# A lane convolution made two units ahead, and its VectorE part moved to one unit ahead

## The chip, the core and the metric

The kernel runs on one core of a Trainium2 chip. The metric is the device time of one execution, in microseconds (us). The kernel before took 767.79 us (median of three runs, 767.70 to 768.71).

The core's engines work side by side and meet through semaphores: TensorE (PE in the profile; its weight loads PEld) multiplies matrices into PSUM accumulators, VectorE (DVE), ScalarE (ACT) and GpSimd (POOL) work element by element, and SyncE (SP) only issues transfers. GpSimd and ScalarE can issue transfers too. Each engine takes its instructions in the order in which the program gives them.

## The reference

```python
# x: (8, 4096, 192); weight: (8 heads, 7 taps); softmax over the taps of each head
out = np.einsum('hk,bskhg->bshg', w, x_unf)     # causal convolution along the sequence, 24 channels a head
x = out.reshape(32768, 192)
gate = np.maximum(x @ w_gate, 0.0)              # 192 -> 1536
val = x @ w_val                                 # 192 -> 1536
return gate * val @ w_out                       # 1536 -> 192, float32
```

Each output token of the convolution is a weighted sum of the token and the six before it, with seven weights for each of the eight heads. Then comes a gated feed-forward layer.

## The kernel before

**Units.** The eight sequences are taken as four pairs; the two of a pair sit on partitions 0 to 63 and 64 to 127, and the 192 channels in three chunks (`c`) of 64. A unit is 1024 tokens of both sequences of a pair, in two windows of 512; there are 16 units. `xc[u]` holds a unit's convolved input in float16, `[128, 3, 1024]`, from a pool of three buffers.

**What TensorE does in a unit.** `gate_val(u, w)` runs once for each window: for each of 12 blocks `f` of 128 hidden channels, twelve matmuls of 512 columns (L505), the gate's into one PSUM tile and the value's into another. ScalarE makes the gate's relu (L516, `gr`), VectorE multiplies it with the value (L517, `hT`). Then `project(u, ...)` multiplies by the output weights. Its four tiles `i` are the two windows by the two sequences. In the normal form a tile is made in two half passes (`half_pass`, L536, `turn` 0 and 1) that use the upper and the lower 64 rows of the array side by side. The second pass of a tile may only start when the first is over; that is passed on by an empty instruction on SyncE's queue:

```python
done = nc.sync.nop()
tc.add_manual_dep(done.ins, mm.ins.name, SYNC, reason="first turn over")
```

The order of the passes (tile, turn) is (0,0) (1,0) (0,1) (2,0) (1,1) (3,0) (2,1) (3,1). After its second pass a tile is evicted from PSUM (L573, by ScalarE; the last tile of a unit by ScalarE and VectorE in halves) and stored by a transfer on SyncE's queue (L574). Unit 0 uses another form: four tiles, each of 48 full-height matmuls (`half_whole`, L556), without the empty instructions. All PSUM tiles come from one pool of four.

**How a unit's convolution is made.** Unit 0 is convolved on TensorE with a dense form (`conv_dense`, L333), unit 1 with banded matmuls (`conv`, L358): a group of up to five blocks of 112 tokens takes eight matmuls of 48 columns a block, five moves by ScalarE out of PSUM (L373) and one transpose on SyncE's queue for each block into `xc[1]` (L395). Units 2 to 15 are made by the "lanes". The lane of a unit `u` is loaded by GpSimd (`lane_load`, L414), copied by GpSimd and turned by nine transposes on SyncE's queue (`lane_turn`, L433 and L436). Tokens 0 to 575 are made by VectorE: ScalarE writes the first tap's product (`lane_first`, L469), VectorE adds the other six taps for each chunk (`lane_rest`, L481, 18 steps, the last three writing `xc`). Tokens 576 to 1023 are GpSimd's: ScalarE and VectorE write the products of tap and token (`product`, L452 and L454), GpSimd adds them in six steps (`add`, L458), the last of which writes `xc`.

**Order.** The schedule is written by hand: the order of the Python calls is each engine's order. In the loop over `u`, the lane of unit `u + 2` is turned, VectorE's 18 steps and the products for unit `u + 2` stand behind the second window's gate and value work and so run during `project(u)`, and GpSimd's adds for unit `u + 1` run during unit `u`. So both parts of a unit are begun two units ahead, VectorE's part is also done two units ahead, and GpSimd's part one. Unit 1's ten blocks are convolved in two groups: group 2 ahead of `project(0)`, group 3 behind its first tile.

Of the kernel before, what the change touches and what calls it, by code (L numbers as in the profile page):

```python
# [8 lines left out]
FP = mybir.dt.float32  # L9
F16 = mybir.dt.float16  # L10
# [5 lines left out]
def kernel(  # L16
# [25 lines left out]
    SUB = 112  # L42
    VECTOR = [
        [(0, 5), (1, 5), (2, 5), (0, 4), (1, 4), (2, 4), (2, 1)],
        [(0, 5), (1, 5), (2, 5), (0, 6), (2, 1)],
    ]
# [11 lines left out]
    second = [min(t, 2 * UNIT - SUB) for t in range(UNIT, 2 * UNIT, SUB)]  # L58
    GROUPS += [(0, second[:GSUB]), (0, second[GSUB:])]
# [3 lines left out]
    xpool = ctx.enter_context(tc.tile_pool(name="xpool", bufs=3))  # L63
# [3 lines left out]
    ypool = ctx.enter_context(tc.tile_pool(name="ypool", bufs=2))  # L67
# [7 lines left out]
    def load_x(g):  # L75


        bp, toks = GROUPS[g]
        xt = xpool.tile([128, GSUB, 2, D], F16, name="x_h")
        rows, step = (SUB, DSUB) if g < 2 else (128, SUB)  # L80
        for st in range(2):
            b = bp + NB * st
            last = toks[-1] - toks[-2] != step
            n_full = len(toks) - int(last)
            src = bass.AP(
                tensor=x.tensor,
                offset=x.offset + (b * S + toks[0] - PAD) * D,
                ap=[[D, rows], [step * D, n_full], [1, D]],
            )
            nc.gpsimd.dma_start(out=xt[0:rows, 0:n_full, st, :], in_=src)  # L90
            if last:
                nc.gpsimd.dma_start(
                    out=xt[0 : SUB + PAD, len(toks) - 1, st, :],
                    in_=x[b, toks[-1] - PAD : toks[-1] + SUB, :],
                )
        return xt
# [305 lines left out]
    def lane_load(u):  # L402


        bp, t0 = u * UNIT // S, u * UNIT % S
        xe = epool.tile([128, TILES, 2, NCH, 64], F16, name="x_e")
        j0 = int(t0 == 0)
        if j0:
            nc.gpsimd.memset(xe[0:HALO, 0, :, :, :], 0.0)
        for st in range(2):  # L410
            b = bp + NB * st
            for j, n in ((j0, TDVE - j0), (TDVE, TILES - TDVE)):
                lo = t0 - HALO + 128 * j if j < TDVE else t0 + LDVE - HALO
                nc.gpsimd.dma_start(  # L414
                    out=xe[:, j : j + n, st, :, :].rearrange("p j c r -> p j (c r)"),
                    in_=bass.AP(
                        tensor=x.tensor,
                        offset=x.offset + (b * S + lo) * D,
                        ap=[[D, 128], [128 * D, n], [1, D]],
                    ),  # L420
                )
            if j0:
                nc.gpsimd.dma_start(
                    out=xe[HALO:128, 0, st, :, :].rearrange("p c r -> p (c r)"),
                    in_=x[b, 0 : 128 - HALO, :],
                )
        xes[u] = xe

    def lane_turn(u):
        xe = xes.pop(u)  # L430
        xp = epool.tile([128, TILES, NCH, 2, 64], F16, name="x_p")
        for st in range(2):
            nc.gpsimd.tensor_copy(out=xp[:, :, :, st, :], in_=xe[:, :, st, :, :])  # L433
        xr = rpool.tile([128, NCH, 128 * TILES], F16, name="x_r")
        for j in range(TILES):
            nc.sync.dma_start_transpose(  # L436
                out=xr[:, :, 128 * j : 128 * j + 128],
                in_=xp[:, j].rearrange("p c s r -> p (c s r)"),
            )
        xrs[u] = xr  # L440

    def shifted(u, c, k, lane):
        o = HALO - KW + 1 + k
        if lane:
            return xrs[u][:, c, 128 * TDVE + o : 128 * TDVE + o + LPOOL]
        return xrs[u][:, c, o : o + LDVE]

    def product(engine, u, c, k):
        out = prods[u][:, k, c, :]
        in_, scale = shifted(u, c, k, 1), tap[:, c, k : k + 1]  # L450
# [5 lines left out]
    def add(u, k):  # L456
        pr = prods[u]
# [7 lines left out]
    def lane_first(u):  # L465
        accs[u] = apool.tile([128, NCH, LDVE], FP, name="acc")
        xc[u] = xcpool.tile([128, NCH, UNIT], F16, name="xc")
        for c in range(NCH):
            nc.scalar.activation(  # L469
                out=accs[u][:, c, :],  # L470
                in_=shifted(u, c, 0, 0),
                func=ACTF.Copy,
                scale=tap[:, c, 0:1],
            )
        prods[u] = apool.tile([128, KW, NCH, LPOOL], FP, name="prods")

    def lane_rest(u):
        acc = accs.pop(u)
        for k in range(1, KW):
            for c in range(NCH):  # L480
                nc.vector.scalar_tensor_tensor(  # L481
                    out=xc[u][:, c, 0:LDVE] if k == KW - 1 else acc[:, c, :],
                    in0=shifted(u, c, k, 0),
                    scalar=tap[:, c, k : k + 1],
                    in1=acc[:, c, :],
                    op0=ALU.mult,
                    op1=ALU.add,
                )
        for c, k in VECTOR[u > 2]:
            product(nc.vector, u, c, k)  # L490
# [62 lines left out]
    def half_whole(h, st, outs):  # L553
        for q in range(4):
            for f in range(NFF):
                nc.tensor.matmul(  # L556
                    out=outs[q],
                    lhsT=h[:, f, st, 128 * q : 128 * (q + 1)],
                    rhs=Wo[:, f, :],
                    start=(f == 0),  # L560
                    stop=(f == NFF - 1),
                )

# [44 lines left out]
    def project(u, hs, work):  # L608
# [3 lines left out]
        if u == 0:  # L612
            order = [(i, 2) for i in range(4)]
        if u == NUNIT - 1:
            order = [(0, 0), (1, 0), (0, 1), (2, 0), (1, 1), (2, 1), (3, 2)]
        for i, turn in order:
            h, st = hs[i // 2], i % 2
            row0 = (bp + NB * st) * S + WIN * (w0 + i // 2)
            if u == NUNIT - 1 and i == 3:
                last_half(h, st, row0)  # L620
                continue
            if turn in (0, 2):
                at[i] = slots()
            if turn in (1, 2):
                for c, k in work[i]:
                    product(nc.scalar, u + 2, c, k)
# [18 lines left out]
    lane_load(2)  # L645
    xts[2] = load_x(2)
    nc.gpsimd.dma_start(out=Wo[:], in_=moe_w_out.rearrange("(c p) d -> p c d", p=128))
    for u in range(NUNIT):
        lane = 1 <= u < NUNIT - 1
        if lane:  # L650
            add(u + 1, 1)
        if u == 1:
            lane_load(3)
            add(2, 2)
            add(2, 3)
# [5 lines left out]
        if u == 0:  # L661
            xts[3] = load_x(3)
        if 0 < u < NUNIT - 3:
            lane_load(u + 3)
        if lane:
            for k in range(4 if u == 1 else 2, KW - 1):
                add(u + 1, k)
        while len(hs) < 2:
            hs.append(gate_val(u, len(hs)))
        if lane:  # L670
            add(u + 1, KW - 1)
        if u == 0:
            xc[1] = xcpool.tile([128, NCH, UNIT], F16, name="xc")
            conv(2, 0)
            conv(2, 1)
        del xc[u]
        work = [[] for _ in range(4)]
        if u + 2 < NUNIT:
            lane_first(u + 2)
            lane_rest(u + 2)  # L680
            todo = [(c, k) for k in (0, 1, 2, 3, 4, 6) for c in range(NCH)]
            todo = [ck for ck in todo if ck not in VECTOR[u > 0]]
            cut = [0, 4, 8, 12, 16] if u == 0 else [0, 5, 10, 15, 16]
            work = [todo[a:b] for a, b in zip(cut, cut[1:])]
# [31 lines left out]
```

## Time and profile before

| | us |
|---|---|
| median of the runs before | 767.79 |
| the profiled execution | 767.88 |
| its span, first to last instruction | 765.9 |
| outside the span | 2.0 |

| engine | busy us | share of the span |
|---|---|---|
| TensorE, matmuls | 761.7 | 99% |
| VectorE | 692.7 | 90% |
| ScalarE | 600.7 | 78% |
| GpSimd | 369.9 | 48% |

A line of the profile gives the engine, the line of kernel.py, the operation, its output and inputs by the program's names, their shapes and the count. In the timeline the first two numbers are the start and the length of a merged row in us, and brackets tell how long the engine was idle before it and what released it. SPq is SyncE's queue of transfers. The ends of matmuls are modelled; they lie about 0.16 us behind the start of the next one.

### The profile page before, as it was taken

The page shows a single profiled execution, that of the slowest core. Times are in us where ns is not written, and L with a number is a line of the kernel's source. Part 1 is how long each engine was busy: PE and PEld are TensorE (multiplying, and loading weights), DVE is VectorE, ACT ScalarE, POOL GpSimd, SP SyncE. Part 2 cuts the span into 40 slices and gives each one's busy share as a digit, 9 for nine tenths or more (in the row PEclk, how much of TensorE's full clock was granted, in tenths as well). Part 3 has the DMA queues.
Part 4 walks back from the last instruction along what each step waited for, and adds up shares of the span by engine and source line. Part 5 has one row for each costly group of instructions (what it writes and reads, how often), then busy time and mean ns, then how long its engine had stood idle before and what let it go on. Part 6 is the DMA issues. An engine that isn't in the chain of part 4 may idle for free.

```text
span 765.9 us, 24782 instructions
## 1 busy us (share of the span) xinstructions
PE 761.7 (99%) x10794; PEld 502.5 (66%) x10794; DVE 692.7 (90%) x746; ACT 600.7 (78%) x735; POOL 369.9 (48%) x212
## 2 busy tenths in 40 slices
PE   9999999999999999999999999999999999999998
PEld 4595674946749476584755848567484674947648
DVE  7999999999999999999999999999999999996591
ACT  6797887878878787887878878788787887875571
POOL 8608648093570926619166290743908346090000
PEclk9999999999999999999999999999999999999999
DMA  8966727190472804528054281722919131200202
GB/s 121 134 104 116 92 91 88 54 122 6 100 78 66 110 23 97 61 85 95 23 111 47 85 92 44 106 31 85 93 44 117 21 92 39 65 22 15 71 2 84
DMA packets 131810, 56.12 MB, mean 73 GB/s; under 512 B 96741, under 2 KB 131701, under 8 KB 131701
## 3 DMA queue, kind: packets, MB, share of 16 engines
q1 hardware_dynamic: 90789, 38.85, 25.1%
q0 software_dynamic: 40768, 15.59, 18.9%
q8 instruction: 84, 1.38, 0.8%
q14 instruction: 25, 0.20, 0.1%
q10 hardware_dynamic: 144, 0.10, 0.0%
HBM read 31.68 MB, written 25.17 MB: 74 GB/s over the span
## 4 chain that ended last, share of the span: by engine, by line
PE 99%; DMA 1%; issue 0%; POOL 0%; ACT 0%; POOLq 0%
PE ps L505 65%; PE ps L536 31%; PE ps L556 2%; DMA x_h<-in_x_dram 1%; PE ps L594 1%; PE ps L333 0%; PE ps L358 0%; POOL spaced L129 0%; ACT acc L573 0%; POOLq L700 0%
## 5 line engine op out<-in xcount | busy, mean ns | idle before, releaser
L517 DVE TENSOR_TENSOR hT<-gr,ps 128x1024 f16<-128x1024 f16 (+1 forms) x386 | 468.9, 1215 | 37.0 <-ACT gr L516 9.9
L516 ACT ACTIVATE gr<-ps 128x1024 f16<-128x1024 f32 (+1 forms) x386 | 392.9, 1019 | 102.4 <-PE ps L505 100.6
L458 POOL TENSOR_TENSOR prods<-prods 128x1344 f32<-128x1344 f32 x70 | 212.4, 3034 | 309.1 <-DVE prods L454 305.7
L505 PE MATMUL ps<-xc,Wg 64*128 64x512 f16 x2304 | 311.9, 376 | 0.0
L505 PE MATMUL ps<-xc,Wv 64*128 64x512 f16 x2304 | 311.8, 376 | 0.0
L536 PEld LDWEIGHTS <-hT 64*128 64x128 f16 x5664 | 234.1, 94 | 3.6
L536 PE MATMUL ps<-Wo,hT 64*128 64x192 f16 x5664 | 236.1, 243 | 0.0
L505 PEld LDWEIGHTS <-Wv 64*128 64x128 f16 x2304 | 129.8, 94 | 118.5 <-DVE hT L517 0.3
L505 PEld LDWEIGHTS <-Wg 64*128 64x128 f16 x2304 | 112.2, 94 | 132.4 <-issue 0.2
L481 DVE SCALAR_TENSOR_TENSOR acc<-x_r,tap,acc 128x576 f32<-128x576 f16 x210 | 154.3, 811 | 1.6 <-ACT acc L469 1.6
L452 ACT ACTIVATE prods<-x_r,tap 128x448 f32<-128x448 f16 x222 | 130.3, 662 | 0.0
L573 ACT COPY out_s<-ps 128x768 f32<-128x768 f32 (+1 forms) x63 | 45.7, 725 | 52.4 <-PE ps L536 42.5
L414 POOL DMA_DIRECT2D x_e<-in_x_dram x56 | 45.1, 818 | 3.4 <-POOL x_p L433 3.4
L433 POOL COPY x_p<-x_e 128x1728 f16<-128x1728 f16 x28 | 44.7, 1624 | 1.7 <-DMA x_e<-in_x_dram 1.6
L458 POOL TENSOR_TENSOR xc<-prods 128x1344 f16<-128x1344 f32 x14 | 42.4, 3027 | 1.1
L481 DVE SCALAR_TENSOR_TENSOR xc<-x_r,tap,acc 128x576 f16<-128x576 f16 x42 | 31.8, 810 | 0.0
L573 DVE COPY out_s<-ps 128x384 f32<-128x384 f32 x15 | 8.3, 550 | 25.5 <-ACT out_s L573 25.5
L469 ACT ACTIVATE acc<-x_r,tap 128x576 f32<-128x576 f16 x42 | 29.4, 766 | 0.0
L454 DVE TENSOR_SCALAR prods<-x_r,tap 128x448 f32<-128x448 f16 x72 | 27.3, 446 | 0.0
L556 PE MATMUL ps<-Wo,hT 128*128 128x192 f16 x192 | 16.2, 246 | 0.0
L556 PEld LDWEIGHTS <-hT 128*128 128x128 f16 x192 | 15.9, 98 | 0.0
L90 POOL DMA_DIRECT2D x_h<-in_x_dram x6 | 4.9, 825 | 0.0
(54 smaller groups left out, 66.9 us busy)
## 6 DMA issues: line engine op xcount, KB each, us to landing
out_dram<-out_s SPq DMA_DIRECT2D x63, 384.0 KB
x_e<-in_x_dram POOLq DMA_DIRECT2D x34, 192.0 KB, 6.2
x_e<-in_x_dram POOLq DMA_DIRECT2D x22, 240.0 KB, 4.8
x_r<-x_p SPq DMA_TRANSPOSE x126
Wo<-in_moe_w_out_dram POOLq DMA_DIRECT2D x1, 576.0 KB
x_h<-in_x_dram POOLq DMA_DIRECT2D x2, 240.0 KB, 7.6
x_h<-in_x_dram POOLq DMA_DIRECT2D x2, 210.0 KB, 5.1
x_h<-in_x_dram POOLq DMA_DIRECT2D x2, 192.0 KB, 7.6
```

The source lines that it names most:

```text
L414: nc.gpsimd.dma_start(out=xe[:, j : j + n, st, :, :].rearrange("p j c r -> p j (c r)"), in_=bass.AP(tensor=x.tensor, offset=x.offset + (b ...
L433: nc.gpsimd.tensor_copy(out=xp[:, :, :, st, :], in_=xe[:, :, st, :, :])
L452: engine.activation(out=out, in_=in_, func=ACTF.Copy, scale=scale)
L458: nc.gpsimd.tensor_tensor(out=pr[:, 0] if k < KW - 1 else xc[u][:, :, LDVE:UNIT], in0=pr[:, 0], in1=pr[:, k], op=ALU.add,)
L469: nc.scalar.activation(out=accs[u][:, c, :], in_=shifted(u, c, 0, 0), func=ACTF.Copy, scale=tap[:, c, 0:1],)
L481: nc.vector.scalar_tensor_tensor(out=xc[u][:, c, 0:LDVE] if k == KW - 1 else acc[:, c, :], in0=shifted(u, c, k, 0), scalar=tap[:, c, k : k ...
L505: nc.tensor.matmul(out=pss[i][:, st, :], lhsT=W[64 * st : 64 * st + 64, c, 128 * f : 128 * (f + 1)], rhs=xcb[64 * st : 64 * st + 64, c, WI ...
L516: nc.scalar.activation(out=gr[:, sts], in_=pss[0][:, sts], func=ACTF.Relu)
L517: nc.vector.tensor_tensor(out=h[:, f, sts], in0=gr[:, sts], in1=pss[1][:, sts], op=ALU.mult)
L536: mm = nc.tensor.matmul(out=outs[q], lhsT=h[64 * r : 64 * r + 64, f, st, 128 * q : 128 * (q + 1)], rhs=Wo[64 * r : 64 * r + 64, f, :], sta ...
L556: nc.tensor.matmul(out=outs[q], lhsT=h[:, f, st, 128 * q : 128 * (q + 1)], rhs=Wo[:, f, :], start=(f == 0), stop=(f == NFF - 1),)
L573: one(out=dst[:, step * j : step * j + step], in_=src[:, step * j : step * j + step])
```

## The change

VectorE's part of a lane now belongs to the next unit, and GpSimd's to the one after it. The lane `v` holds tokens 0 to 575 of unit `v` and tokens 576 to 1023 of unit `v + 1`. In the loop over `u` lane `u + 1` is turned and worked on, so VectorE's part of unit `u + 1` is made during `project(u)`, and the products for GpSimd's part of unit `u + 2` too. GpSimd's adds in unit `u` make unit `u + 1`'s part, as before. Lanes run from 1 to 15; the last has no GpSimd part. On TensorE only tokens 576 to 1023 of unit 1 are convolved, in one group of four blocks. It is called in `project(0)` behind pass (1,1). Unit 0's projection takes the form of half passes that the other units have.

GpSimd's copies and SyncE's transposes of a lane are made for VectorE's five blocks first and then for GpSimd's four. The output weights are loaded ahead of unit 1's input. Two pools shrink: `xpool` from three buffers to two, `ypool` from two to one. The products that VectorE makes are the same five in each unit.

```diff
-    VECTOR = [
-        [(0, 5), (1, 5), (2, 5), (0, 4), (1, 4), (2, 4), (2, 1)],
-        [(0, 5), (1, 5), (2, 5), (0, 6), (2, 1)],
-    ]
+    VECTOR = [(0, 5), (1, 5), (2, 5), (0, 6), (2, 1)]
...
-    second = [min(t, 2 * UNIT - SUB) for t in range(UNIT, 2 * UNIT, SUB)]
-    GROUPS += [(0, second[:GSUB]), (0, second[GSUB:])]
+    GROUPS += [(0, list(range(UNIT + LDVE, 2 * UNIT, SUB)))]
...
-    def lane_load(u):
+    def pieces(v):
+        both = [(0, TDVE, v * UNIT)]
+        if v + 1 < NUNIT:
+            both.append((TDVE, TILES - TDVE, (v + 1) * UNIT + LDVE))
+        return both
...
+    def lane_turn(v):
+        xe = xes.pop(v)
+        xp = epool.tile([128, TILES, NCH, 2, 64], F16, name="x_p")
+        xr = rpool.tile([128, NCH, 128 * TILES], F16, name="x_r")
+        for j0, n, _ in pieces(v):
+            for st in range(2):
+                nc.gpsimd.tensor_copy(
+                    out=xp[:, j0 : j0 + n, :, st, :], in_=xe[:, j0 : j0 + n, st, :, :]
                 )
...
+            for j in range(j0, j0 + n):
+                nc.sync.dma_start_transpose(
+                    out=xr[:, :, 128 * j : 128 * j + 128],
+                    in_=xp[:, j].rearrange("p c s r -> p (c s r)"),
+                )
+        xrs[v] = xr
...
-            out=pr[:, 0] if k < KW - 1 else xc[u][:, :, LDVE:UNIT],
+            out=pr[:, 0] if k < KW - 1 else xc[v + 1][:, :, LDVE:UNIT],
...
-        if u == 0:
-            order = [(i, 2) for i in range(4)]
...
-            if turn == 2:
-                half_whole(h, st, at[i][1])
-            else:
-                done[i] = half_pass(h, st, at[i][1], turn, done.get(i))
+            done[i] = half_pass(h, st, at[i][1], turn, done.get(i))
             if turn:
-                evict(at[i][0], row0, u > 0 and i == 3 or u == NUNIT - 1 and i == 2)
-            if u == 0 and i == 0:
-                conv(3, 0)
-                conv(3, 1)
+                evict(at[i][0], row0, i == 3 or u == NUNIT - 1 and i == 2)
+            if u == 0 and (i, turn) == (1, 1):
+                conv(2, 0)
+                conv(2, 1)
...
-    lane_load(2)
+    lane_load(1)
+    nc.gpsimd.dma_start(out=Wo[:], in_=moe_w_out.rearrange("(c p) d -> p c d", p=128))
     xts[2] = load_x(2)
-    nc.gpsimd.dma_start(out=Wo[:], in_=moe_w_out.rearrange("(c p) d -> p c d", p=128))
     for u in range(NUNIT):
-        lane = 1 <= u < NUNIT - 1
-        if lane:
-            add(u + 1, 1)
...
+        adds = 1 <= u < NUNIT - 1
+        if u + 1 < NUNIT:
+            xc[u + 1] = xcpool.tile([128, NCH, UNIT], F16, name="xc")
+        if adds:
+            add(u, 1)
         hs = []
         if u == 0:
             hs.append(gate_val(0, 0))
+        if u + 1 < NUNIT:
+            lane_turn(u + 1)
         if u + 2 < NUNIT:
-            lane_turn(u + 2)
...
+            lane_load(u + 2)
+        if adds:
+            for k in range(2, KW):
+                add(u, k)
         while len(hs) < 2:
             hs.append(gate_val(u, len(hs)))
...
-            conv(2, 0)
-            conv(2, 1)
         del xc[u]
         work = [[] for _ in range(4)]
+        if u + 1 < NUNIT:
+            lane_first(u + 1)
+            lane_rest(u + 1)
         if u + 2 < NUNIT:
-            lane_first(u + 2)
-            lane_rest(u + 2)
...
         project(u, hs, work)
```

More of the change, by code (lines that the diff above doesn't have):

```diff
@@ L78, in load_x @@
         bp, toks = GROUPS[g]
+        n, rows, step = len(toks), SUB if g < 2 else 128, toks[1] - toks[0]
         xt = xpool.tile([128, GSUB, 2, D], F16, name="x_h")
-        rows, step = (SUB, DSUB) if g < 2 else (128, SUB)
         for st in range(2):
-            b = bp + NB * st
-            last = toks[-1] - toks[-2] != step
-            n_full = len(toks) - int(last)
             src = bass.AP(
                 tensor=x.tensor,
-                offset=x.offset + (b * S + toks[0] - PAD) * D,
-                ap=[[D, rows], [step * D, n_full], [1, D]],
-            )
[L90 to L95, printed above, removed]
+                offset=x.offset + ((bp + NB * st) * S + toks[0] - PAD) * D,
+                ap=[[D, rows], [step * D, n], [1, D]],
+            )
+            nc.gpsimd.dma_start(out=xt[0:rows, 0:n, st, :], in_=src)
         return xt
@@ L414, in lane_load @@
+    def lane_load(v):
+        xe = epool.tile([128, TILES, 2, NCH, 64], F16, name="x_e")
+        for j0, n, t in pieces(v):
+            bp, t0 = t // S, t % S
+            start = int(t0 == 0)
+            if start:
+                nc.gpsimd.memset(xe[0:HALO, j0, :, :, :], 0.0)
+            for st in range(2):
+                b = bp + NB * st
                 nc.gpsimd.dma_start(
-                    out=xe[:, j : j + n, st, :, :].rearrange("p j c r -> p j (c r)"),
+                    out=xe[:, j0 + start : j0 + n, st, :, :].rearrange("p j c r -> p j (c r)"),
@@ L442, in shifted @@
[L442 removed]
+                        offset=x.offset + (b * S + t0 - HALO + 128 * start) * D,
+                        ap=[[D, 128], [128 * D, n - start], [1, D]],
+                    ),
+                )
+                if start:
+                    nc.gpsimd.dma_start(
+                        out=xe[HALO:128, j0, st, :, :].rearrange("p c r -> p (c r)"),
+                        in_=x[b, 0 : 128 - HALO, :],
+                    )
+        xes[v] = xe
+    def lane_turn(v):
[3 more added lines that the diff above has]
+        for j0, n, _ in pieces(v):
+            for st in range(2):
+                nc.gpsimd.tensor_copy(
+                    out=xp[:, j0 : j0 + n, :, st, :], in_=xe[:, j0 : j0 + n, st, :, :]
+                )
+            for j in range(j0, j0 + n):
+                nc.sync.dma_start_transpose(
+                    out=xr[:, :, 128 * j : 128 * j + 128],
+                    in_=xp[:, j].rearrange("p c s r -> p (c s r)"),
+                )
+        xrs[v] = xr
@@ L443, in shifted, with product @@
+    def shifted(v, c, k, lane):
         o = HALO - KW + 1 + k
         if lane:
[L445 to L450, printed above, removed]
+            return xrs[v][:, c, 128 * TDVE + o : 128 * TDVE + o + LPOOL]
+        return xrs[v][:, c, o : o + LDVE]
+    def product(engine, v, c, k):
+        out = prods[v][:, k, c, :]
+        in_, scale = shifted(v, c, k, 1), tap[:, c, k : k + 1]
@@ L463, in add, with lane_first @@
         )
-    def lane_first(u):
-        accs[u] = apool.tile([128, NCH, LDVE], FP, name="acc")
-        xc[u] = xcpool.tile([128, NCH, UNIT], F16, name="xc")
+    def lane_first(v):
+        accs[v] = apool.tile([128, NCH, LDVE], FP, name="acc")
         for c in range(NCH):
             nc.scalar.activation(
-                out=accs[u][:, c, :],
-                in_=shifted(u, c, 0, 0),
+                out=accs[v][:, c, :],
+                in_=shifted(v, c, 0, 0),
                 func=ACTF.Copy,
@@ L474, in lane_first, with lane_rest @@
             )
-        prods[u] = apool.tile([128, KW, NCH, LPOOL], FP, name="prods")
-    def lane_rest(u):
-        acc = accs.pop(u)
+    def lane_rest(v):
+        acc = accs.pop(v)
         for k in range(1, KW):
@@ L481, in lane_rest @@
                 nc.vector.scalar_tensor_tensor(
-                    out=xc[u][:, c, 0:LDVE] if k == KW - 1 else acc[:, c, :],
-                    in0=shifted(u, c, k, 0),
+                    out=xc[v][:, c, 0:LDVE] if k == KW - 1 else acc[:, c, :],
+                    in0=shifted(v, c, k, 0),
                     scalar=tap[:, c, k : k + 1],
@@ L488, in lane_rest @@
                 )
-        for c, k in VECTOR[u > 2]:
-            product(nc.vector, u, c, k)
+        if v + 1 < NUNIT:
+            prods[v] = apool.tile([128, KW, NCH, LPOOL], FP, name="prods")
+            for c, k in VECTOR:
+                product(nc.vector, v, c, k)
     def gate_val(u, w):
@@ L551, in half_pass @@
             return done
[L553 to L562, printed above, removed]
     def put(copy, queue, src, row, n, gap, os_=None):
```

61 lines of the change are left out of this document (9 added, 52 removed).

## The prediction

> **What bounds the kernel now.** I read the page first (busy shares, the chain that ended last), then the chain in order of time, then the timelines of the engines around unit 0 and around unit 3, which stands for units 1 to 14.
>
> Page, parts 1 and 4:
>
> ```profile
> PE 761.7 (99%) x10794; PEld 502.5 (66%) x10794; DVE 692.7 (90%) x746; ACT 600.7 (78%) x735; POOL 369.9 (48%) x212
> PE 99%; DMA 1%; issue 0%; POOL 0%; ACT 0%; POOLq 0%
> ```
>
> TensorE is never without work: what lengthens or shortens its own chain is the whole answer, and everything else matters only if it makes TensorE wait. The chain in order of time (start, length, what) gives its stages:
>
> ```profile
> 21.57 19.56 PE ps L505 x180
> 41.13 0.99 PE ps L358 x8
> 42.12 3.96 PE ps L556 x48
> 46.09 0.82 PE ps L358 x8
> 46.91 11.88 PE ps L556 x144
> 58.79 31.19 PE ps L505 x288
> ...
> 183.81 15.84 PE ps L536 x384
> 199.66 31.08 PE ps L505 x288
> ```
>
> A unit is 31.08 us of gate and value matmuls (L505) and 15.84 us of projection (L536), 46.92 together, with no hole. Unit 0 differs: its projection is 3.96 + 11.88 in full-height matmuls (L556), with the two convolutions (L358, 0.99 and 0.82) between; from 41.13 to 58.79 that is 17.66 us. This stretch is what the change rewrites.
>
> **Units 1 to 15: a new wait, with cover.** VectorE's rows are now made in the unit before they are read, so the first gate matmuls of a unit wait for the last VectorE steps of the unit before. Timelines of VectorE and TensorE where unit 3 ends:
>
> ```profile
> 196.35 2.27 DVE L481 SCALAR_TENSOR_TENSOR xc<-x_r,tap,acc 128x576 f16<-128x576 f16 x3
> 199.49 0.81 PE L505 MATMUL ps<-xc,Wg 64*128 64x512 f16 x6
> ```
>
> The three final steps (one for each 64-channel chunk) end between 197.16 and 198.62. TensorE starts the next unit at 199.49 and comes to the third chunk four matmuls (0.43 us) later, at 199.92. The cover is 2.3 us for the first chunk and 1.30 for the third, in all units alike, since VectorE's order within a unit stays (15 + 3 steps, five products, half an eviction). I cost this wait at nothing. Behind it would stand all of TensorE; a lag beyond 1.30 us would be paid at each of 15 boundaries. Unit 14 gets 18 steps for unit 15 (13.3 us) where VectorE idled (14.77 us before its eviction, by its timeline). GpSimd's adds come in the same unit as before; its two copies of 1.62 us become four of 0.9 or 0.7, in a unit in which it waits over 20 us.
>
> **Start.** The loads keep their places on GpSimd's queue, but the output weights now go ahead of unit 1's input: they are needed at 41, were issued at 24.68, and the move brings them forward. The unit-1 input is needed ten us later than before. Nothing here is on the chain.
>
> **Unit 0, step by step.** I set 0 where the projection starts, and take ScalarE's times from its timeline of unit 3 (projection from 183.65; evictions of the first and second tile):
>
> ```profile
> 189.80 0.80 ACT L573 COPY out_s<-ps 128x768 f32<-128x768 f32 x1 [0.77 <-PE ps L536]
> 193.76 0.80 ACT L573 COPY out_s<-ps 128x768 f32<-128x768 f32 x1 [0.36 <-PE ps L536]
> ```
>
> The eight passes of a projection take 15.84 / 8 = 1.98 us each.
>
> *Convolution.* Sixteen matmuls of 240 columns (0.99 + 0.82 us) become eight of 192: 0.82 x 192/240 = 0.66 to 0.79, taken as 0.75. Half passes instead of full-height matmuls cost the same (15.84 both). On TensorE alone the stretch is 15.84 + 0.75 = 16.6: 1.1 less than 17.66.
>
> *The accumulator of the fourth tile.* The convolution's two accumulators come between the third and the fourth tile's, and there are four in all, so pass (3,0) now gets the second tile's and waits for its eviction. The second tile's pass (1,1) ends at 9.90, the convolution at 10.65, the eviction (193.76 + 0.80, less 183.65) at 10.91. (3,0) starts at about 11.0: 0.35 lost. (3,0) ends at 12.98, (2,1) at 14.96.
>
> *SyncE's queue.* This is the item that decides. Pass (3,1) may start only when SyncE has passed on the end of (3,0), by the empty instruction that `half_pass` puts on its queue. Between that and the instruction before it now stand the convolution's four transposes (`conv` is called behind pass (1,1), and `nc.sync` issues in order). Unit 0 had no such instruction before, as it used `half_whole`. What a transpose costs SyncE, and that what stands behind it waits, its timeline of unit 0 shows:
>
> ```profile
> 43.74 6.92 SPq L395 DMA_TRANSPOSE xc<-y  x5
> 50.76 0.53 SPq L574 DMA_DIRECT2D out_dram<-out_s  x1
> 51.39 8.21 SPq L395 DMA_TRANSPOSE xc<-y  x5
> 59.71 1.86 SPq L574 DMA_DIRECT2D out_dram<-out_s  x3
> ```
>
> The answer for line 395 (shortest/median/longest, ns) and ScalarE's timeline of the same unit:
>
> ```profile
> L395 SPq DMA_TRANSPOSE xc<-y x10: 1174/1246/1814, 43.7 to 58.4; - x10
> ```
>
> ```profile
> 47.82 0.81 ACT L573 COPY out_s<-ps 128x768 f32<-128x768 f32 x1
> 48.49 2.03 ACT L373 CAST y<-ps 112x480 f16<-112x480 f32 x5
> ```
>
> The first tile was evicted at 48.63, and its store, though ready, went out at 50.76, right behind five transposes; the later stores sat behind the second five until 59.71. So the queue is strictly in order, and a transpose holds it for 1.17 to 1.81 us. Stores could wait; TensorE can't.
>
> In the changed kernel ScalarE starts the five moves out of the convolution 0.69 after the start of the second eviction (48.49 - 47.82): at 10.80. They took 2.03 for 480 columns; for 384, 1.62: done at 12.45. Four transposes then take 5.1 at the median with 0.05 between, 5.7 with one of the long ones. Both groups of before had one of 1.81 among their first four, so I take 5.6: until 18.05. Another 0.1 to the next instruction of the queue (43.74 + 6.92 to 50.76), and as much again to TensorE, an estimate: (3,1) starts at 18.25 instead of 14.96, and ends at 20.23.
>
> *Sum.* 20.23 - 17.66 = +2.6; counted from starts of matmuls (41.0 to 58.72) it is +2.5. So 1.1 us of removed matmuls is paid back by 0.35 and 3.3 us of stall. Low end: median transposes, +2.0. High end: if unit 1's rows are turned no earlier than unit 2's were (the first product then at 45.58, and not 2.48 behind the start, at 43.5), ScalarE, with 0.36 to spare before the second eviction, is 1.7 late: +4.2. I take no lateness, since VectorE's five blocks are now loaded and copied first, so that SyncE can begin about two copies (1.8 us) after 25.7 rather than at 30.7. In the longer projection VectorE's rows for unit 1 (42.8 + 13.3 = 56.1) are in time; the convolved rows are read only in the second window, 15 us later.
>
> Nothing else moves the chain. The profiled execution took 767.88 (span 765.9), 0.09 above the median of the three runs, 767.79. 767.88 + 2.5 is 770.4; as a median 770.3.
>
> **Rivals.**
>
> *TensorE's clock falls in the stall.* Between (2,1) and (3,1) there are 3.3 us without a matmul. Before, no hole of this kind exists between 8 us and the end. At the very start the trace shows a slow pace:
>
> ```profile
> 0.86 2.83 PE L157 MATMUL ps<-const-bfloat16-1.0 128*128 128x512 bf16 x7 [0.86 <-PEq L700]
> ```
>
> Six matmuls of 512 columns and one of 128 take 2.83, 0.45 for 512 columns, where the gate has 31.08 / 144 = 0.216 for a pair that runs side by side. A further one at 4.09 is still 0.45 from the next start, 4.54; so some four us went at half pace, two us lost. The same after the stall would make it +4.5, 772.3. Against it: the hole is short, and there would be one only; the granted clock column reads 1.00 even at the start, so it tells nothing. [...]
>
> *The transposes don't hold (3,1): not slower.* If SyncE were through by 14.96, only the 0.35 would remain: 9.90 + 0.75 + 0.35 + 5.94 = 16.9, -0.7, a median of 767.1. That needs four transposes in 14.96 - 12.45 = 2.5 us, 0.63 each, about half of the shortest row, 1.17; above that every us more is a us of TensorE. [...] That the change doesn't do what it says is no way to this: the program's order has eight convolution matmuls of 192 columns, and the four transposes before the third store.
>
> *VectorE comes late at each boundary.* The price is 15 times what goes beyond 1.30 us: at 0.3 us over, +4.5, on top of the +2.5, 774.8. Against it stands that the ends repeat to 0.1 us in all units before.
>
> **How the numbers follow.** Stall in unit 0 as summed (769.8 to 772.0 with its bounds): 0.77. With the clock's fall: 0.08. Transposes hidden: 0.08. VectorE late: 0.03. Something not seen: 0.04, of it 0.03 faster. A measurement of this kernel can tell about 0.2%, 1.5 us, from no change; 770.3 is +0.33%, and the low end of the sum +0.26%. Slower: 0.77 + 0.08 + 0.03, less 0.03 for a stall shorter than its low end, 0.85. Same: 0.08 + 0.03 + 0.01 = 0.12. Faster: 0.03. The range leaves out the hidden transposes and the late VectorE: 769.2 to 772.4.
>
> **What would show it.** In the profile after: 46.92 us for units 1 to 14; in unit 0 one idle time of TensorE of some 3.3 us ahead of the last pass, released by SyncE, with four transposes on SyncE until just before it; 20.2 us from gate to gate there. No such hole, and the unit at 16.9, would prove the queue harmless; matmuls at twice their length behind the hole, the clock; a gate start that waits for VectorE, the third rival.

## The result and the profile after

The changed kernel took 775.22 us (median of five runs, 774.47 to 775.57) beside 768.18 for the kernel before on the same chip: the ratio is 1.0085, with an interval of 1.0074 to 1.0096. It is slower, as forecast, but by 7.0 us and not 2.5, and 2.8 us above the top of the range. The profiled execution took 774.75, span 772.9 (before: 767.88 and 765.9).

Parts 1 and 4 of the page of the changed kernel:

```profile
PE 763.0 (99%) x10978; PEld 506.0 (65%) x10978; DVE 705.4 (91%) x763; ACT 601.7 (78%) x735; POOL 374.3 (48%) x240
PE 91%; DMA 3%; SPq 2%; POOL 2%; ACT 1%; issue 0%; POOLq 0%; ACTq 0%
```

The busy shares hardly moved; the second line did. TensorE's chain is broken now, and what precedes the break is a path of transfers and queues. The chain in order of time (start, length, what) shows it:

```profile
39.98 8.91 DMA x_r<-x_p
49.00 2.91 ACT prods L448 x5
52.59 2.81 ACT prods L448 x5
56.07 1.56 ACT y L361 x5
58.88 1.75 SPq L383
60.69 1.24 SPq L383
61.98 1.25 SPq L383
63.34 2.16 PE ps L532 x48
65.50 31.08 PE ps L501 x288
96.58 15.84 PE ps L532 x384
```

From 65.50 on all is as before: 31.08 + 15.84 = 46.92 a unit. Unit 1's first gate matmul starts at 65.33 (58.72 before), so 6.6 of the 7.0 us of span are lost ahead of it. The stretch from the start of unit 0's projection to that matmul takes 65.33 - 40.81 = 24.5 us; it was 17.7, and 20.2 was forecast. The chain names two things: the last transpose of lane 1's rows (`x_r`), 8.91 us from its issue to its landing, and three of the four convolution transposes on SyncE's queue (L383).

The timeline of the same stretch, ScalarE, TensorE and SyncE (start, length; in brackets the idle time before and its releaser):

```profile
49.00 2.91 ACT L448 ACTIVATE prods<-x_r,tap 128x448 f32<-128x448 f16 x5 [3.25 <-DMA x_r<-x_p]
51.81 0.78 ACT L558 COPY out_s<-ps 128x768 f32<-128x768 f32 x1
52.63 0.49 PE L346 MATMUL ps<-x_h,band 118*112 118x192 f16 x4 [1.10 <-ACT out_s L558]
55.30 0.78 ACT L558 COPY out_s<-ps 128x768 f32<-128x768 f32 x1
56.12 5.79 PE L532 MATMUL ps<-Wo,hT 64*128 64x192 f16 x96 [3.00 <-ACT out_s L558]
57.66 5.57 SPq L383 DMA_TRANSPOSE xc<-y  x4
63.34 2.16 PE L532 MATMUL ps<-Wo,hT 64*128 64x192 f16 x48 [1.43 <-SPq L545]
```

ScalarE waits for lane 1's rows until 49.00 (the forecast had its first product at 43.5). They are the lane's last four blocks, from which the products for unit 2 are made; GpSimd adds nothing of them before 59.62. But `project` calls these products ahead of the evictions, so on ScalarE both evictions stand behind them (they start at 51.81 and 55.30, right behind five products each), and TensorE waits for the accumulators: 1.10 us in the middle of the convolution, 3.00 ahead of pass (3,0). The forecast hole ahead of (3,1), released by SyncE, is there too, but only 1.43 us long, since (3,0) and (2,1) are late themselves. And these two passes take 5.79 instead of 4.14 (the same row in e1, below). The windows view tells why (window, its length, then each engine's busy time, the granted clock, the share of the DMA engines, GB/s):

```profile
56.12:59.50 3.38, 3.38 (x46) 3.37 (x47) 3.35 (x8) 3.38 (x9) 0.00 (x0) 0.54 0.51 147
63.34:65.33 1.99, 1.99 (x48) 1.99 (x50) 0.00 (x0) 0.00 (x0) 1.99 (x4) 1.00 0.65 186
```

Behind the hole of 3.00 TensorE was granted 0.54 of its clock and did 46 matmuls in 3.38 us; at 1.00 it did 48 in 1.99. So the clock column does show this fall, which the prediction doubted. It lasted 3.41 us in the records, from 56.40 to 59.82. Whether it costs anything here is asked in e7.

Why the rows were late is shown by GpSimd's timelines of 30 to 35 us, before and after:

```profile
30.64 0.76 POOL L90 DMA_DIRECT2D x_h<-in_x_dram  x1
31.38 0.56 POOL L92 DMA_DIRECT2D x_h<-in_x_dram  x1
31.93 0.77 POOL L90 DMA_DIRECT2D x_h<-in_x_dram  x1
32.68 0.56 POOL L92 DMA_DIRECT2D x_h<-in_x_dram  x1
```

```profile
31.39 3.19 POOL L407 DMA_DIRECT2D x_e<-in_x_dram  x4 [0.30 <-POOL x_p L428]
```

Before, this place had four loads of 192 + 192 + 44 + 44 = 472 KB; the lane of unit 3 was loaded only in unit 1. Now `lane_load(2)` stands here, 2 x 240 + 2 x 192 = 864 KB. The windows of 40 to 45 us, before and after:

```profile
40.00:45.00 5.00, 5.00 (x57) 4.29 (x52) 3.23 (x4) 4.56 (x10) 0.00 (x0) 1.00 0.56 99
```

```profile
40.00:45.00 5.00, 5.00 (x112) 4.62 (x110) 3.07 (x4) 2.50 (x5) 0.00 (x0) 1.00 1.49 165
```

The last two columns are the DMA share and GB/s. Before, GpSimd's loads were over at 39.2 by the trace, and the last of the nine transposes landed at 44.7, 1.1 us behind the end of its issue. After, the loads ran until 47.9, beside the transposes (DMA share 1.49 in this window, against 0.56 before), and the last transpose landed at 48.9, 6.8 us behind. The profile of before has both cases in itself: its first transpose, issued while loads still ran, landed 6.6 us behind the end of its issue (32.0 to 38.6).

### The profile page after: what moved, and what is told of

Its sections match the earlier page's. It is cut to its first block, busy times and chain, and to the rows that moved or that the text cites. A ratio compares the mean times of both kernels' runs of the same rounds, so it can differ in the third digit from the quotient of the medians.

```text
span 772.9 us, 25195 instructions
## 1 busy us (share of the span) xinstructions
PE 763.0 (99%) x10978; PEld 506.0 (65%) x10978; DVE 705.4 (91%) x763; ACT 601.7 (78%) x735; POOL 374.3 (48%) x240
## 4 chain that ended last, share of the span: by engine, by line
PE 91%; DMA 3%; SPq 2%; POOL 2%; ACT 1%; issue 0%; POOLq 0%; ACTq 0%
PE ps L501 60%; PE ps L532 31%; SPq L432 1%; DMA x_r<-x_p 1%; DMA x_e<-in_x_dram 1%; ACT prods L448 1%; DMA Wg<-in_moe_w_gate_dram 1%; SPq L383 1%; PE ps L579 1%; POOL Wg L168 0%; POOL Wg L161 0%; POOL Wv L161 0%; POOL x_e L407 0%; POOL x_h L83 0%; ACT y L361 0%
## 5 line engine op out<-in xcount | busy, mean ns | idle before, releaser
L532 PE MATMUL ps<-Wo,hT 64*128 64x192 f16 x6048 | 254.3, 244 | 4.4 <-ACT out_s L558 3.0
L532 PEld LDWEIGHTS <-hT 64*128 64x128 f16 x6048 | 251.6, 95 | 8.7 <-issue 3.2
L475 DVE SCALAR_TENSOR_TENSOR acc<-x_r,tap,acc 128x576 f32<-128x576 f16 x225 | 165.3, 811 | 1.8 <-ACT acc L464 1.8
L428 POOL COPY x_p<-x_e 128x960 f16<-128x960 f16 (+1 forms) x58 | 50.3, 905 | 0.7 <-DMA x_e<-in_x_dram 0.7
L407 POOL DMA_DIRECT2D x_e<-in_x_dram x58 | 47.0, 822 | 3.6 <-POOL x_p L428 3.3
L475 DVE SCALAR_TENSOR_TENSOR xc<-x_r,tap,acc 128x576 f16<-128x576 f16 x45 | 34.0, 811 | 0.0
L464 ACT ACTIVATE acc<-x_r,tap 128x576 f32<-128x576 f16 x45 | 31.4, 764 | 2.2 <-DMA x_r<-x_p 2.2
L168 POOL COPY Wg<-Wg 64x768 f16<-64x768 f16 (+1 forms) x4 | 3.6, 901 | 3.0 <-DMA Wg<-in_moe_w_gate_dram 2.9
L145 PE MATMUL ps<-const-bfloat16-1.0 128*128 128x512 bf16 (+1 forms) x10 | 3.9, 526 | 0.9 <-PEq L670 0.9
L321 PEld LDWEIGHTS <-x_h 110*32 110x32 f16 (+3 forms) x240 | 3.2, 93 | 1.6 <-issue 1.3
```

The costliest lines, as they stand in the source:

```text
L407: nc.gpsimd.dma_start(out=xe[:, j0 + start : j0 + n, st, :, :].rearrange("p j c r -> p j (c r)"), in_=bass.AP(tensor=x.tensor, offset=x.of ...
L428: nc.gpsimd.tensor_copy(out=xp[:, j0 : j0 + n, :, st, :], in_=xe[:, j0 : j0 + n, st, :, :])
L464: nc.scalar.activation(out=accs[v][:, c, :], in_=shifted(v, c, 0, 0), func=ACTF.Copy, scale=tap[:, c, 0:1],)
L475: nc.vector.scalar_tensor_tensor(out=xc[v][:, c, 0:LDVE] if k == KW - 1 else acc[:, c, :], in0=shifted(v, c, k, 0), scalar=tap[:, c, k : k ...
L532: mm = nc.tensor.matmul(out=outs[q], lhsT=h[64 * r : 64 * r + 64, f, st, 128 * q : 128 * (q + 1)], rhs=Wo[64 * r : 64 * r + 64, f, :], sta ...
```

## The experiments

The theory from these readings: the early load makes lane 1's rows late, SyncE's queue holds pass (3,1), and the clock falls in the holes. The first four kernels (e1 to e4) were timed beside 767.93 for before, the next four beside 768.11, the last beside 768.43. Diffs are against the changed kernel unless said.

**The load moved out of unit 0** (e1), so that nothing but SyncE's queue should be left.

```diff
+        if u == 1:
+            lane_load(2)
+            add(1, 2)
+            add(1, 3)
...
-        if u + 2 < NUNIT:
+        if 0 < u < NUNIT - 2:
             lane_load(u + 2)
...
-            for k in range(2, KW):
+            for k in range(4 if u == 1 else 2, KW):
```

> Only the load of lane 2 is moved: out of unit 0 into unit 1, behind GpSimd's first add, where the kernel before had its second lane load. Theory (that load shares the transfer engines with the nine transposes of lane 1, which land until 48.8 us in the changed kernel, and ScalarE's products wait for them from 45.8 to 49.0): the transposes land by 44.6, the first product starts between 43.4 and 44.6, the second eviction ends between 51.6 and 52.5, SyncE's hold ahead of pass (3,1) now shows in full, about 3 us, and unit 1's gate starts between 61.0 and 61.8: 770.5 to 771.6 us, or 773 if TensorE's clock falls in that hole. Rival (SyncE's queue is the main cost and ScalarE is late for another reason): the products still start near 49 and the time stays at 775.

Measured: 772.34 (770.69 to 774.03, five runs), ratio 1.0056 [1.0043, 1.0069]: 2.9 under the changed kernel. Its timeline:

```profile
43.23 2.90 ACT L448 ACTIVATE prods<-x_r,tap 128x448 f32<-128x448 f16 x5
50.87 0.80 ACT L558 COPY out_s<-ps 128x768 f32<-128x768 f32 x1 [0.36 <-PE ps L532]
51.72 4.14 PE L532 MATMUL ps<-Wo,hT 64*128 64x192 f16 x96
53.27 6.29 SPq L383 DMA_TRANSPOSE xc<-y  x4
59.68 3.59 PE L532 MATMUL ps<-Wo,hT 64*128 64x192 f16 x48 [3.83 <-SPq L545]
```

```profile
59.27:62.68 3.41, 3.00 (x38) 2.89 (x40) 0.00 (x0) 0.00 (x0) 3.41 (x4) 0.50 0.61 145
```

This is the kernel that the prediction described. The projection starts at 40.75; counted from there the first product comes at 2.48 (forecast 2.48), (3,0) at 10.97 (11.0), (3,1) at 18.93 (18.25). The four transposes took 6.29 us, 5.6 forecast. Then comes the rival in place of the forecast: the clock is at 0.50 for the 3.41 us from 59.27, and (3,1) takes 3.59 instead of the 2.16 of its row above. That rival was priced at 772.3. Each run also comes with its mean granted clock: 3.41 us at half clock are 1.7 us or 0.2% of the span, so a run with such a fall reads 0.998 or less. Four of e1's five runs read 0.997 or 0.998 and took 772.3 to 774.03; the one at 0.999 took 770.69, close to the 770.3 of the forecast.

**The four transposes moved behind the empty instruction** (e2); the load stays early.

```diff
+
+    def conv_turn(g):
+        bp, toks = GROUPS[g]
+        y = convs[g]
         for jj, t in enumerate(toks):
...
             done[i] = half_pass(h, st, at[i][1], turn, done.get(i))
+            if u == 0 and (i, turn) == (3, 0):
+                conv_turn(2)
```

> Only the four transposes of the convolution are moved on SyncE's queue, behind the empty instruction for pass (3,0). Theory (the late lane transposes set the time, SyncE's hold adds only what is left of it): TensorE's wait of 1.4 us ahead of pass (3,1) goes, and nothing else: 773.8. Rival (SyncE's queue is the main cost): 771 or less.

Measured: 769.13 (768.0 to 771.55, eleven runs), 1.0015 [1.0006, 1.0025]. The rival's side: I had read the small hole ahead of (3,1) in the profile, 1.43, as all that SyncE's queue cost, and the order on it was worth 6.1 of medians. Not all of the 6.1 is the queue's: in this profile the products stand 5.9 us behind the projection's start and in the first one of the changed kernel 8.2, for which the order on SyncE's queue gives no reason. The profile (the slowest of the eleven runs) still has late rows and a fall of the clock:

```profile
47.77 2.90 ACT L452 ACTIVATE prods<-x_r,tap 128x448 f32<-128x448 f16 x5 [1.96 <-DMA x_r<-x_p]
54.89 7.77 PE L536 MATMUL ps<-Wo,hT 64*128 64x192 f16 x144 [2.15 <-ACT out_s L562]
```

The 144 matmuls of the last three passes take 6.12 at full clock (e3 and e4, below); here 1.65 more.

**The same, and 30 matmuls of 128 columns behind the convolution**, into columns that nothing reads (e3), to keep TensorE at work in the hole.

```diff
+        if part == 1:
+            for _ in range(30):
+                nc.tensor.matmul(
+                    out=ps[:, 0, 384:512], lhsT=busy[:, 0:128], rhs=busy[:, 0:128], start=True, stop=True
+                )
```

> As the run with the transposes behind, and thirty dummy matmuls of 128 columns, whose output nobody reads, behind the convolution, to fill the 3.0 us in which TensorE waits for the second eviction. Theory (after that hole the granted clock is 0.5 for 3.4 us, which makes passes (3,0) and (2,1) 1.8 us longer): the clock stays at 1.0, the two passes take 3.96 instead of 5.8, and the time is 1.8 below that run, 772.0. Rival (the two passes are long for another reason, such as waits on their inputs): as that run, 773.8.

Measured: 769.09 (768.24 to 770.48, eleven runs), 1.0016 [1.0007, 1.0025], against e2's 769.13: no gain in the median, a smaller spread. In its profile the three passes run at 6.12 behind a hole of 0.29. The median run of e2 showed a clock of 1.0, so there was nothing to win in it; only two of e2's eleven runs read 0.997 (770.75 and 771.55), and none of e3's reads less than 0.999.

**Both moves, e1 and e2 together** (e4).

> The late load of lane 2 and the transposes behind the empty instruction together. Theory: with ScalarE in time, SyncE's hold is worth its full 3.3 us, so this is 3.3 below the run with the late load alone; unit 0's projection is 16.6 to 17.3 us from gate to gate: 767.2 to 768.0 us, the same as the kernel before or up to 1 us faster. Rival (a wait that is not yet seen stands behind both): 770 or more.

Measured: 767.29 (766.73 to 768.76, eleven runs), 0.9993 [0.9984, 1.0002]. As expected.

```profile
50.92 0.80 ACT L562 COPY out_s<-ps 128x768 f32<-128x768 f32 x1 [0.36 <-PE ps L536]
51.77 6.12 PE L536 MATMUL ps<-Wo,hT 64*128 64x192 f16 x144
57.71 0.83 PE L505 MATMUL ps<-xc,Wg 64*128 64x512 f16 x6
```

From the projection's start at 40.80 to 57.71 it is 16.9 us, with only the accumulator's wait left; the convolution and that wait take 0.96 (from its start at 50.81 to 51.77). The four medians side by side:

| | transposes ahead of the empty instruction | behind it |
|---|---|---|
| lane 2 loaded in unit 0 | 775.22 (changed kernel) | 769.13 (e2) |
| lane 2 loaded in unit 1 | 772.34 (e1) | 767.29 (e4) |

The queue costs 5.05 us alone, the load 1.84 alone, both together 7.9. The 5.05 are the hole ahead of (3,1) and, in four of e1's five runs, the fall of the clock behind it; none of e4's runs reads less than 0.999.

**The early load alone, in the kernel before** (e5, diff against before): does it delay transposes there too?

```diff
-            lane_load(3)
...
+            lane_load(3)
```

The first line stood in unit 1; the second stands in unit 0, behind `load_x(3)`.

> The kernel before, with one edit: its second lane load (lane 3) is issued in unit 0, behind the load of the fourth convolution group, instead of in unit 1. Theory (a load of 864 KB issued while the first lane's transposes are in flight delays their landing): the last transpose lands at 48 to 51 instead of 44.6, ScalarE's products start 3 to 6 us later than 45.6, the first tile is evicted 3 to 6 us later than 47.8, the third tile waits for its accumulator, and the time is 769.5 to 772. Rival (the lateness in the changed kernel has to do with the new lane or its order of copies): the transposes land by 45 and the time stays at 768.0.

Measured: 771.05 (770.2 to 771.76, five runs), 1.0032 [1.002, 1.0045]: one load of the kernel before, issued earlier, costs 2.9 us. By the trace unit 2's rows landed at 49.5 instead of 44.7, and the path is the same:

```profile
49.59 2.35 ACT L452 ACTIVATE prods<-x_r,tap 128x448 f32<-128x448 f16 x4 [2.52 <-DMA x_r<-x_p]
52.67 8.08 PE L556 MATMUL ps<-Wo,hT 128*128 128x192 f16 x96 [1.93 <-ACT out_s L573]
```

**Half of the load** (e6): e2 with only VectorE's five blocks of lane 2, 480 KB, in unit 0.

```diff
+        if u == 1:
+            lane_load(2, slice(1, 2))
...
-            lane_load(u + 2)
+            lane_load(u + 2, slice(0, 1) if u == 0 else slice(0, 2))
```

> As the run with the transposes behind, but only VectorE's five blocks of lane 2 (480 of 864 KB) are loaded in unit 0; GpSimd's four follow in unit 1. Theory: the lateness goes with the amount, so the last lane transpose lands between 41.8 (nothing loaded) and 47.4 (all loaded), about 44 to 45, the first product starts 3 to 5 us behind the start of the projection, against 2.5 and 5.9, and the time is between 767.3 and 769.1. Rival (any load there costs the whole): as the run with the whole load, 769.1.

Measured: 767.26 (766.45 to 768.44, eleven runs), 0.9986 [0.9978, 0.9995], the same as with no load (e4). The rows landed at 44.3, so the first product came 3.25 behind the projection's start:

```profile
44.38 2.91 ACT L450 ACTIVATE prods<-x_r,tap 128x448 f32<-128x448 f16 x5
47.29 0.80 ACT L560 COPY out_s<-ps 128x768 f32<-128x768 f32 x1
51.25 0.80 ACT L560 COPY out_s<-ps 128x768 f32<-128x768 f32 x1 [0.36 <-PE ps L534]
```

The first eviction starts right behind the products, 6.16 behind the projection's start as in e4; before the second ScalarE idles again. Here the delay of 0.77 us (3.25 against e1's 2.48) is swallowed by ScalarE's slack; of the 5.7 in the first profile after, 1.4 was (the balance, below).

**The 30 matmuls in the changed kernel itself** (e7): is the clock's fall on the path?

> The changed kernel with the thirty dummy matmuls behind the convolution and nothing else. Theory: the fall of the clock after the first hole lies beside SyncE's hold, so that keeping the clock there ends pass (2,1) 1.8 us earlier but pass (3,1) starts when SyncE lets it; the hole ahead of it grows from 1.7 to some 3.3 us and the clock may fall behind that one: 773.5 to 775.5, no gain. Rival (the fall of the clock is on the path): 773.4 or less.

Measured: 772.5 (771.54 to 775.77, six runs), 1.0058 [1.0041, 1.0075]: 2.7 under the changed kernel's first runs and 1.5 under its second (e9, below; there the intervals overlap), where my theory had no gain. The time is on the rival's side; the profile is not:

```profile
46.82 2.90 ACT L453 ACTIVATE prods<-x_r,tap 128x448 f32<-128x448 f16 x5 [2.30 <-DMA x_r<-x_p]
53.95 4.14 PE L537 MATMUL ps<-Wo,hT 64*128 64x192 f16 x96 [0.15 <-ACT out_s L563]
55.49 5.07 SPq L388 DMA_TRANSPOSE xc<-y  x4
60.68 2.15 PE L537 MATMUL ps<-Wo,hT 64*128 64x192 f16 x48 [2.58 <-SPq L550]
```

With (3,0) and (2,1) at full pace the hole ahead of (3,1) is longer, 2.58, and no fall follows it. The four transposes begin 8.67 us behind the first product, and (3,1) starts 0.12 behind the last of them; in the first profile of the changed kernel, where the clock fell, it was 8.66 and 0.11. So the fall there lies beside SyncE's hold and only shortens the hole ahead of (3,1), as my theory had it. What parts the two profiles from the projection's start to the next gate, 24.5 and 21.8 us, is rows 2.2 us less late and transposes 0.5 us shorter, not the clock. Why the medians differ stays open.

**The convolution at the start of the projection** (e8, diff against e4), so that its accumulators are free long before (3,0).

```diff
+        if u == 0:
+            conv(2, 0)
+            conv(2, 1)
...
-            if u == 0 and (i, turn) == (1, 1):
-                conv(2, 0)
-                conv(2, 1)
```

> Late load of lane 2, transposes behind, and the convolution's matmuls and moves ahead of unit 0's first pass, so that no tile waits for another's eviction. Theory: the wait of 0.34 us ahead of pass (3,0) goes and the moves delay VectorE's rows of unit 1 by 1.7 us, to the edge of their cover: 0.3 below the run with late load and transposes behind, 766.9, which is 1.0 us or 0.13% below the kernel before. Rival (VectorE's rows now come too late for unit 1's gate): 767.5 to 769, with a wait of TensorE for VectorE at the start of unit 1.

Measured: 767.01 (766.76 to 768.71, twelve runs), 0.9985 [0.9977, 0.9994]: 1.1 us under the kernel before, 8.2 under the changed one. The projection has no hole:

```profile
41.79 16.01 PE L536 MATMUL ps<-Wo,hT 64*128 64x192 f16 x384
57.64 0.81 PE L505 MATMUL ps<-xc,Wg 64*128 64x512 f16 x6
```

From e4 to e8 0.28 of the medians and 0.14 of the stretch (57.64 - 40.87 = 16.77) went with the accumulator's wait. The delay of VectorE that I expected did not come: ScalarE takes the accumulators' products ahead of the moves.

**The changed kernel once more** (e9), since in its first profile the products stood 8.2 us behind the projection's start, and in e2, e3 and e7, with the same loads, 5.9.

> The changed kernel itself, once more, with a profile of its own. In its first profile the first product for VectorE came 8.2 us behind the start of unit 0's projection, in the kernels that move the four convolution transposes or add idle matmuls (with the same loads) 5.9 us behind. If that difference is only how late the transfers in flight happen to land in one execution, the products stand 5.5 to 8.5 us behind here too, at another place within that band than 8.2, the hole ahead of pass (3,1) is 1.5 to 3.3 us, and the two holes ahead of and behind passes (3,0) and (2,1) make 4.0 to 5.0 us together, with one fall of the clock (3.4 us at half pace); median 774 to 776. If the lateness of 8.2 belongs to this order of SyncE's queue, the first product stands at 8.0 to 8.4 again.

Measured: 774.04 (772.49 to 775.2, four runs), 1.0078 [1.0061, 1.0095]. The profiled execution, at 772.49 the fastest of them:

```profile
46.46 2.90 ACT L448 ACTIVATE prods<-x_r,tap 128x448 f32<-128x448 f16 x5 [1.70 <-DMA x_r<-x_p]
53.58 5.79 PE L532 MATMUL ps<-Wo,hT 64*128 64x192 f16 x96 [1.86 <-ACT out_s L558]
55.12 5.89 SPq L383 DMA_TRANSPOSE xc<-y  x4
61.13 2.15 PE L532 MATMUL ps<-Wo,hT 64*128 64x192 f16 x48 [1.76 <-SPq L545]
63.12 0.81 PE L501 MATMUL ps<-xc,Wg 64*128 64x512 f16 x6
```

Here the products are 5.6 behind the start (40.85), so the lateness is a matter of the execution. The two holes make 3.6, less than the 4.0 I had put as the least, and the median of 774.04 lies within what I expected. The first product came 2.54 us earlier than in the first profile, and the span is 2.2 us shorter. The four runs read 0.998, 1.000, 0.996 and 0.995; the one without a fall took 773.49, no less than the profiled one with it.

## Why the prediction was right or wrong

*Right.* Units 1 to 14 keep 46.92 us: VectorE's cover holds, and neither the start nor the tail adds more than some 0.4 us. The sum in unit 0 stands almost term for term once the load is out of the way: the convolution and the accumulator's wait were put at 0.75 + 0.35 = 1.10 and take 0.96 in e4; from the projection's start to the next gate, "transposes hidden" was worked out as 16.9 us and 767.1, and e4, where they are hidden, has 16.9 and 767.29. That queue order makes (3,1) wait was right, and its size nearly: the hole was put at 3.3 and is 3.83 in e1 (4.0 from start to start of matmuls, as the forecast counted), as the transposes took 6.29 and not 5.6.

*Wrong:* the step that failed is "I take no lateness". It asked only when SyncE could begin to issue lane 1's transposes, the five for VectorE first, while ScalarE's products read the four behind them. In what it asked it was right: SyncE began earlier than before (28.77, against 30.72) and was through with the ninth at 42.1. The step took the issue for the landing. The price of `lane_load(2)`, which the change moves into unit 0, was missing in the sum: 864 KB beside the transposes. From the projection's start, the products stood 8.2 - 2.5 = 5.7 us late in the first profile and 3.1 in the second; the high end allowed for ScalarE being 1.7 late. The last of unit 2's transposes in the profile of before, on which that end rested, landed when the loads were over. e5 shows the mechanism without any other part of the change (the rows landed at 49.5 instead of 44.7), e6 that half of the load does no harm (767.26, against 767.29 with none in e4). The traces give the size: 6.8 us from the end of the last transpose's issue to its landing beside the load (after), 1.1 without it (before).

*The balance.* The path from the projection's start to the next gate, in us; the last column is the sum:

| | to the first product | to the first of the four transposes | the four | to (3,1) | to the gate | |
|---|---|---|---|---|---|---|
| forecast | 2.48 | 9.97 | 5.6 | 0.2 | 1.98 | 20.2 |
| first profile after | 8.19 | 8.66 | 5.57 | 0.11 | 1.99 | 24.5 |
| second (e9) | 5.61 | 8.66 | 5.89 | 0.12 | 1.99 | 22.3 |
| e1 | 2.48 | 10.04 | 6.29 | 0.12 | 3.43 | 22.4 |

In the first profile the products are 5.7 late. ScalarE's idle times take up 10.04 - 8.66 = 1.4 of it (the prediction gave it 0.36 to spare), and SyncE begins 4.4 later than forecast; all else on the path is as forecast within 0.1. So the lateness of the rows is the whole of the 4.3. The fall of the clock is not on this path, but in e1 it is: its pass (3,1) takes 3.43 to the gate.

*Half right:* the fall of the clock, given a chance of 0.08. It came far more often: all five runs of the changed kernel read 0.997 or 0.998, and three of four in its second set 0.998 or less. The argument against it ("the hole is short, and there would be one only") was wrong. But the forecast had it behind the hole ahead of (3,1), and the profiles of the changed kernel have it ahead of (3,0), where it is hidden by SyncE's hold; in e1 it is where the forecast put it, and costs 1.43 us where two were priced. That the hole was short was no argument: the clock fell at holes of 1.86, 2.15 and 3.00 us too, all shorter than the 3.3 worked out, and did not at one of 2.58 (last section).

*Open.* How late the rows land was seen in single profiles only (8.2 and 5.6 in the changed kernel itself), and why it differs from execution to execution isn't known, so the medians can't be split exactly. Two runs of e9 read 0.995 and 0.996, less than any profiled run; a second fall, behind the hole ahead of (3,1), would be on the path there, but no profile shows one. One of e7's runs reads 0.996, too, and took 775.77, 3.3 above its median; its other five read 0.999 or 1.000. That e1 and e2 do not add up (5.05 + 1.84 = 6.9, measured 7.9 with the first set of runs of the changed kernel and 6.8 with the second) is within this scatter. An order with the evictions ahead of unit 2's products on ScalarE, which would take the late rows off TensorE's path, was not run.

## What to carry to other kernels

When a load moves earlier, ask which transfers are in flight there and who waits for their landing; the issue being early said nothing here (SyncE began 1.95 us earlier than before, and the last transpose landed 4.2 us later). A signal that one engine sent to itself through a queue that also issues transposes inherited their issue time (6.29 us for four, a hole of 3.83, e1), so put the signal ahead of them; here that order was worth 5 us, the fall of the clock included. At holes of TensorE of 1.86 to 3.83 us the clock fell here to half for 3.41 us in four profiles and did not in two (1.93 and 2.58), so count the price of such a hole with and without; then ask whether another wait lies beside the slow stretch and hides it.

## What the runs showed of the hardware that was not expected

The granted clock fell to half at holes of 1.86 (e9), 2.15 (e2), 3.00 (first profile after) and 3.83 us (e1), for 3.41 us where the records give it. It did not fall at 1.93 (e5) or 2.58 (e7), nor at the second holes of 1.43 and 1.76 in the changed kernel. The length alone does not decide. The nearest two are in these windows, of e9 and of e5:

```profile
51.73:53.58 1.85, 0.00 (x0) 0.02 (x1) 1.85 (x3) 1.85 (x5) 0.00 (x0) 1.00 0.30 95
53.58:56.99 3.41, 3.41 (x46) 3.40 (x47) 3.41 (x7) 3.41 (x9) 0.00 (x0) 0.53 0.50 145
```

```profile
50.75:52.66 1.91, 0.00 (x0) 0.00 (x0) 1.91 (x4) 1.91 (x5) 0.00 (x0) 1.00 0.18 36
52.67:60.00 7.33, 7.33 (x89) 7.33 (x89) 7.33 (x13) 7.33 (x15) 0.00 (x0) 1.00 0.35 88
```

Two holes of almost the same length: behind the first TensorE gets 0.53 of its clock and does 46 matmuls of 192 columns in 3.41 us, behind the second it keeps 1.00.

What decides is not shown by these profiles. By the records the half clock begins 0.28 us behind the end of the hole in the first profile after (at 56.40), 0.32 behind it in e2 (55.21) and 0.21 in e9 (53.79); in e1 it begins 0.41 us ahead of the end of the hole (59.27).

A transpose of one block of a lane took SyncE 1.18 to 3.18 us to issue in the profile of before and 1.18 to 2.94 in the first profile after (median 1.26 in both). From the end of its issue to its landing it was 1.1 us when the loads were over (the last of lane 2's nine before), and 6.6 and 6.8 us beside GpSimd's loads (the first of the same nine before, the last of lane 1's nine after).
